# One plain load moved in front of three transposing transfers in the head of a GeGLU feed-forward kernel

## Chip, cores and metric

The kernel runs on one core of one Trainium2 chip. The metric is device time in microseconds (us), the median of several executions. The span of the profile is about 2 us shorter than that time.

## The reference

```python
# x: 32 x 32 x 1024 (1024 tokens), w_gate, w_up: 1024 x 3584, w_down: 3584 x 1024, all bf16
def reference(x, w_gate, w_up, w_down):
    return (gelu_tanh(x @ w_gate) * (x @ w_up)) @ w_down
```

## The kernel before

The kernel replaces matrix products by Strassen-like schemes with seven products. x is kept transposed in four quarters, b11, b12, b21, b22. VectorE (DVE) makes four sums of them, t1 to t4, and TensorE (PE) multiplies quarters and sums of x with quarters and sums of the weights; the sums of weight quarters are s1 to s4.

Until the first sum is there, PE works on "products ahead": gate rows (the tiles a12a and a12b) times b21, for six groups of four, results parked in SBUF. All but three of the earliest transfers of the head go through one queue, the sync engine's (SP). Its later part:

```python
for i in (0, 1):
    load_ahead(i, KQ, KD)
def load_halves(i):
    for k in range(0, KD, KQ):
        load_ahead(i, k, k + KQ)

load_halves(2)                 # gate rows of groups 2 to 4, 512 KB each in two loads
load_halves(3)
for which in (1, 0):
    load_w_all(0, which)       # w_up and w_gate of chunk 0
load_halves(4)
load_xT(0, 0, KD)              # b11: transposing transfer, 512 KB
load_xT(1, 0, KD)              # b12
load_ahead(5, 0, KD)           # gate rows of group 5, 512 KB, one plain load
load_xT(1, KD, DT)             # b22
for which in (1, 0):
    load_w_all(1, which)
```

The part that consumes them:

```python
group_ahead(4, "BBCC")
tt(t1, b12, b11, SUB)                                  # DVE
begun = []
for fl in range(FC):                                   # first product of chunk 0 reads b11
    psa = acc("A")
    prod(psa, quads(0, fl)[0], b11, True)
    begun.append((psa, added(ahead_at[fl], psa)))      # "c" on DVE
tt(t2, b22, t1, SUB)
group_ahead(5, "CCBB", between=lambda: nc.scalar.copy(b22r, b22))
...
tt(t3, b22, b12, SUB)
next(chunk0)                                           # s3 on DVE
tt(t4, b21, t2, SUB)
...
for ci in range(NCH):                                  # chunks of two feature tiles
    ...
    prod(psc[fl], s1[fl], t1, True)                    # needs t1
    ...
    prod(psa[fl], s2[fl], t2, False)                   # needs t2
    ...
    for st in open_fts:
        last_product(st)                               # adds on in the bank psa of the chunk before
    ...
    prod(psc[fl], s4[fl], b22r, False)
    h1.append(gelu(added(sn2[fl], psc[fl]), "h1", 2))  # "c" on DVE reads psc
    ...
    prod(psa[fl], s3[fl], t3, False)
    tt(g_of(ft)[:, NB:], added(sn5[fl], psa[fl]), h1[fl], MUL)   # "c" on DVE reads psa
```

In the text, c is the result of an `added`, and a bank is the piece of memory that a product adds up in (psA, psB or psC).

## Time and profile before

| | before |
|---|---|
| time, median of 3 at first | 274.03 us (273.82 to 274.19) |
| span of the profile | 272.0 us |
| PE busy | 266.5 us, 98% |
| last wait of PE for a transfer | ends at 4.70 us |

The page of the kernel before. In part 1 each engine has its busy time, share and number of instructions; part 4 gives shares of the chain of waits that ended last.

```profile
span 272.0 us, 3354 instructions
...
PE 266.5 (98%) x1182; PEld 191.4 (70%) x1198; DVE 193.3 (71%) x204; ACT 112.9 (41%) x185; POOL 118.6 (44%) x60
...
PE 97%; DMA 1%; issue 0%; ACT 0%; SPq 0%
```

The reader sees a kernel bound by PE. The chain's single DMA piece is the first weight tile.

The timeline of the kernel before on the sync queue: start, length of the issue, operation, tile. The length is the time in which the queue was busy or held up with issuing, not the transfer (the issue at 17.67 takes 0.58 us; its rows landed at 22.88).

```profile
8.95 2.08 SPq L208 DMA_DIRECT2D a12b<-in_w_gate_dram  x2
11.07 6.55 SPq L215 DMA_TRANSPOSE b<-in_x_dram  x2
17.67 0.58 SPq L208 DMA_DIRECT2D a12b<-in_w_gate_dram  x1
18.30 4.29 SPq L215 DMA_TRANSPOSE b<-in_x_dram  x1
22.64 0.58 SPq L135 DMA_DIRECT2D wu<-in_w_up_dram  x1
```

The timeline of the kernel before on DVE. The bracket gives the idle time in front and what ended it.

```profile
21.62 2.29 DVE L342 TENSOR_TENSOR t<-b,b 128x2048 fp32r<-128x2048 bf16 x1 [1.87 <-DMA b<-in_x_dram]
23.83 1.28 DVE L300 TENSOR_TENSOR c<-ahead,psA 128x512 f32<-128x512 f32 x2
25.03 2.29 DVE L348 TENSOR_TENSOR t<-b,t 128x2048 fp32r<-128x2048 bf16 x1
...
38.99 0.67 DVE L300 TENSOR_TENSOR c<-sn,psA 128x512 f32<-128x512 f32 x1
```

DVE waits 1.87 us for b12, then starts t1 (L342) and t2 (L348). There is no other bracket before 43 us: one delay of t1 moves all of this. The last line is the second `added` of chunk 0 that reads psA; it ends at 39.66.

The chain of the kernel before, in order of time: start, length, what.

```profile
25.93 1.73 PE psB L281 x8
27.66 1.85 PE psC L270 x8
29.50 1.82 PE psA L270 x8
```

At 27.66 the products with t1 start, at 29.50 those with t2. Nothing but PE stands there, so in this execution PE does not wait for a transfer there.

### The profile page before, as it was taken

Reading aid. Unit: us, or ns where it says so; the run is one execution under the profiler, and the core shown is the slowest. Engines: PE = TensorE matmul, PEld = TensorE weight load, DVE = VectorE, ACT = ScalarE, POOL = GpSimd, SP = SyncE. Lnnn points to the kernel's source line nnn. Section 1 sums busy time; section 2 is a strip of 40 time slices with the busy share of each in tenths; the row PEclk is TensorE's granted clock in tenths of the full one; section 3 lists DMA queues with packets and bytes.
Section 4 is the critical chain, followed back from the end, with each engine's and each line's share of the span. In section 5 each row is a group of like instructions: output and inputs, shape, how many; then the busy total and the mean of one; then the engine's idle time right before and its main releaser. Section 6 shows DMA issues by size and latency. Waiting matters only on the chain.

```text
span 272.0 us, 3354 instructions
## 1 busy us (share of the span) xinstructions
PE 266.5 (98%) x1182; PEld 191.4 (70%) x1198; DVE 193.3 (71%) x204; ACT 112.9 (41%) x185; POOL 118.6 (44%) x60
## 2 busy tenths in 40 slices
PE   7999999999999999999999999999999999999995
PEld 4444777877877878778778776764447888888883
DVE  1448998786685676765855556459999999999511
ACT  2435765355454643654546436430300023972001
POOL 1090099989787796796786966000000000000000
PEclk9999999999999999999999999999999999999999
DMA  7999130540523504505225090005992435686202
GB/s 170 324 263 254 32 113 15 145 133 23 157 68 86 155 17 140 142 12 157 84 72 154 22 322 7 0 2 157 350 302 80 138 132 186 219 280 205 78 0 77
DMA packets 55888, 35.86 MB, mean 132 GB/s; under 512 B 9792, under 2 KB 55872, under 8 KB 55872
## 3 DMA queue, kind: packets, MB, share of 16 engines
q1 hardware_dynamic: 52496, 33.10, 42.5%
q10 hardware_dynamic: 3376, 2.56, 2.9%
q8 instruction: 9, 0.15, 0.2%
q14 instruction: 7, 0.06, 0.1%
HBM read 31.72 MB, written 2.10 MB: 124 GB/s over the span
## 4 chain that ended last, share of the span: by engine, by line
PE 97%; DMA 1%; issue 0%; ACT 0%; SPq 0%
PE psA L270 37%; PE psC L270 19%; PE psA L419 18%; PE psC L419 7%; PE psB L419 7%; PE psB L281 3%; PE psC L281 3%; PE psA L281 2%; DMA a12a<-in_w_gate_dram 1%; PE psB L270 1%; ACT o_sb L559 0%; SPq L197 0%; PE tp L261 0%
## 5 line engine op out<-in xcount | busy, mean ns | idle before, releaser
L270 PE MATMUL psA<-t,s 128*128 128x512 f32 x224 | 58.3, 402 | 0.0
L245 ACT ACTIVATE h<-c 128x512 bf16<-128x512 f32 x56 | 34.3, 629 | 39.3 <-DVE c L300 39.3
L270 PEld LDWEIGHTS psA<-t,s 128*128 128x128 f32 x224 | 42.1, 188 | 9.9
L170 POOL TENSOR_TENSOR s<-wu 128x1024 fp32r<-128x1024 bf16 x13 | 29.4, 2262 | 32.7 <-DMA wu<-in_w_up_dram 28.3
L171 POOL TENSOR_TENSOR s<-s,wg 128x1024 fp32r<-128x1024 f32 x14 | 30.1, 2147 | 14.8 <-PE psA L270 13.7
L173 POOL TENSOR_TENSOR s<-wg,wu 128x1024 fp32r<-128x1024 bf16 x13 | 28.9, 2223 | 0.0
L270 PE MATMUL psC<-t,s 128*128 128x512 f32 x112 | 27.9, 391 | 0.0
L270 PE MATMUL psA<-t,a22r 128*128 128x512 f32 x112 | 27.9, 391 | 0.0
L270 PE MATMUL psC<-b22r,s 128*128 128x512 f32 x112 | 27.7, 389 | 0.0
L270 PE MATMUL psA<-b,wg 128*128 128x512 bf16 x102 | 25.6, 380 | 0.4
L305 ACT COPY sn<-psC 128x512 f32<-128x512 f32 x28 | 16.3, 588 | 23.3 <-PE psC L270 15.9
L270 PEld LDWEIGHTS psC<-t,s 128*128 128x128 f32 x112 | 21.0, 188 | 4.5
L270 PEld LDWEIGHTS psA<-t,a22r 128*128 128x128 f32 x112 | 21.0, 188 | 4.4
L270 PEld LDWEIGHTS psC<-b22r,s 128*128 128x128 f32 x112 | 21.0, 188 | 4.4
L300 DVE TENSOR_TENSOR c<-sn,psC 128x512 f32<-128x512 f32 x28 | 19.1, 687 | 6.6 <-PE psC L270 6.6
L300 DVE TENSOR_TENSOR c<-sn,psA 128x512 f32<-128x512 f32 x28 | 19.1, 682 | 6.4 <-PE psA L270 6.4
L318 DVE TENSOR_TENSOR hi<-h,psA 128x512 bf16<-128x512 bf16 x14 | 9.6, 688 | 18.0 <-PE psA L270 18.0
L270 PEld LDWEIGHTS <-wg 128*128 128x128 bf16 x128 | 11.4, 98 | 15.5 <-issue 3.7
L172 POOL TENSOR_TENSOR s<-wg,s 128x1024 fp32r<-128x1024 bf16 x10 | 21.5, 2150 | 0.8
L305 ACT COPY sn<-psA 128x512 f32<-128x512 f32 x32 | 18.4, 590 | 7.2 <-PE psA L270 7.1
L300 DVE TENSOR_TENSOR c<-ahead,psA 128x512 f32<-128x512 f32 x24 | 16.3, 686 | 3.7 <-PE psA L270 2.5
L398 DVE TENSOR_TENSOR lo<-c,h 128x512 bf16<-128x512 f32 x14 | 17.9, 1275 | 0.5
(90 smaller groups left out, 381.0 us busy)
## 6 DMA issues: line engine op xcount, KB each, us to landing
wu<-in_w_up_dram SPq DMA_DIRECT2D x14, 512.0 KB, 3.9
wdb<-in_w_down_dram SPq DMA_DIRECT2D x12, 512.0 KB, 4.7
wg<-in_w_gate_dram SPq DMA_DIRECT2D x9, 512.0 KB, 5.1
wdb<-in_w_down_dram SPq DMA_DIRECT2D x12, 384.0 KB, 4.3
v<-in_w_down_dram SPq DMA_DIRECT2D x4, 512.0 KB, 6.4
out_dram<-o_sb ACTq DMA_DIRECT2D x16, 128.0 KB, 1.7
a12b<-in_w_gate_dram SPq DMA_DIRECT2D x6, 256.0 KB, 5.5
wg<-in_w_gate_dram SPq DMA_DIRECT2D x6, 256.0 KB, 4.6
```

Source lines behind the costliest of these rows:

```text
L170: yield engs[0].tensor_tensor(s1, a21, a22, ADD)
L171: yield engs[1].tensor_tensor(s2, s1, a11, SUB)
L172: yield engs[2].tensor_tensor(s4, a12, s2, SUB)
L173: yield engs[3].tensor_tensor(s3, a11, a21, SUB)
L245: nc.scalar.activation(h, src, ACT.Gelu_apprx_tanh)
L270: nc.tensor.matmul(ps, lhsT=lhs[:, k, :], rhs=rhs[:, k, :], start=(start and k == 0), stop=(k == KD - 1), skip_group_check=True,)
L281: nc.tensor.matmul(ps[:, cols], lhsT=a12_ahead[i][:, k, j * P : (j + 1) * P], rhs=b21[:, k, cols], start=(k == 0 and not cols.start), stop ...
L300: tt(t, s, ps, ADD)
L305: nc.scalar.copy(t, ps)
L318: tt(g_of(ft)[:, :NB], h0, psa, MUL)
L398: tt(g_of(ft)[:, NB:], added(sn5[fl], psa[fl]), h1[fl], MUL)
L419: nc.tensor.matmul(banks[m], lhsT=lhs(k)[:, m * P : (m + 1) * P], rhs=rhs(k), start=(start and k == 0), stop=(k == HF - 1), skip_group_che ...
```

## The change

The intent is to let the gate rows of the products ahead load in one stretch, and then the three transposes of x follow each other.

```diff
+        def load_halves(i):
+            for k in range(0, KD, KQ):
+                load_ahead(i, k, k + KQ)
+
         def load_xT(nb, d0, d1):
 ...
-        def load_halves(i):
-            for k in range(0, KD, KQ):
-                load_ahead(i, k, k + KQ)
-
         load_halves(2)
         load_halves(3)
 ...
         load_halves(4)
+        load_ahead(5, 0, KD)
         load_xT(0, 0, KD)
         load_xT(1, 0, KD)
-        load_ahead(5, 0, KD)
         load_xT(1, KD, DT)
```

Only the sync queue's order differs. The instruction orders of PE, DVE, ACT and POOL are the same in both kernels.

## The prediction

> **What bounds the kernel now.** TensorE (PE). The page shows it busy 266.5 of 272.0 us (98%) at a granted clock of 9 tenths or more everywhere. The chain of waits has one DMA in it, the first weight tile until 4.65 us; from 4.70 to 268.83 us every piece is a matmul, apart from "issue" crumbs of 0.05 us. So a reordering of the head's transfers has no PE wait to remove. It can only use up slack.
>
> **What the change moves.** The streams of PE, VectorE (DVE), ACT and POOL are the same. On the sync queue one plain 512 KB load (gate rows of group 5) moves from third to first of four issues; the transposing transfers b11, b12, b22 then follow each other. Moving `load_halves` only moves a definition. Nothing is added or removed.
>
> Times before, from the timeline and the semaphore landings in the trace:
> - b11 issued 11.07, landed 17.71; PE uses it at 22.48.
> - b12 issued 15.72, landed 21.52, which ends DVE's idle time (1.87 us) before t1. 15 of its 16 completions came by 20.00; the last is 1.5 us late, just after a 16 KB packet of the instruction queue at 19.36 that took 1.12 us.
> - group 5's rows issued 17.67, landed 22.88; used at 24.20.
> - b22 issued 18.30, landed 24.65; t2 uses it at 25.03, the ACT copy b22r at 26.45.
>
> **Cost.** The DMA engines are saturated from 8 to 19 us (windows: 290 to 350 GB/s). 512 KB in front of b11 is about 1.5 us at that rate (estimate). I expect group 5's rows to land near 17.5, b11 near 19.2, b12 at 21.4 to 23.0[...], b22 at 23 to 24.7. [...]b12, group 5's rows and b22 landed in order of issue.
>
> **Critical path.** If b12 lands later by d, DVE, which runs without a gap from t1 at 21.62 to about 43 us, shifts by d. PE needs: t1 (ends 23.91, used 27.66, slack 3.7), t2 (ends 27.32, used 29.50, slack 2.1), t3 and s3 (end 29.5 and 30.65, used near 34.95), the psC banks freed by the adds at 33.90 (first ends 34.59, used 36.73, slack 2.1), chunk 1's s1 (slack 2.7), t4 (ends 32.86, used 40.35). The smallest slack is 2.1 us; I expect d of 0 to 1.5 us. So none of it reaches PE, and nothing is gained.
>
> **Prediction: 274.05 us, 273.6 to 274.6 eight times in ten.** Faster by over 2%: 0.3%; within 2%: 99.4%; slower by over 2%: 0.3%.
>
> **What would show the steps right.** The chain is again pure PE from 4.7 us on; the first fp32r products of psC (s1 by t1) and psA (s2 by t2) start at 27.7 and 29.5 as before; group 5's rows land 4 to 6 us earlier; b11 1 to 2 us later; t1 starts 0 to 1.5 us after 21.62; b22 lands no later. Wrong: a PE idle entry with DVE's t or a DMA as releaser, or t1 earlier than 21.5.
>
> **What would make it wrong.** d over 2.1 us: if the slow instruction packet hits b11 and the following transposes wait for it, b12 lands near 23.6 to 24 and PE stalls some tenths of a us at 29.5 or 36.7, below 0.5% of the time. The other way: [...]t1 might start earlier, which still gives PE nothing.

## The result, and the profile after

| | before | after |
|---|---|---|
| time, median of 6 | 273.92 us (273.42 to 274.50) | 274.13 us (273.54 to 274.46) |
| ratio, 95% interval | | 1.0006 (0.9988 to 1.0024) |
| span | 272.0 us | 272.1 us |

A ratio is the mean time of one kernel's fast runs over that of the other's of the same rounds, so it is not quite the ratio of the medians quoted here. The two kernels are the same within 0.25%.

The page of the kernel after:

```profile
span 272.1 us, 3354 instructions
...
PE 267.2 (98%) x1182; PEld 192.0 (71%) x1198; DVE 197.2 (72%) x204; ACT 112.3 (41%) x185; POOL 119.8 (44%) x60
...
PE 98%; issue 0%; ACT 0%; DVE 0%
```

The timeline of the kernel after on the sync queue and, in the next fence, on DVE:

```profile
9.46 2.53 SPq L208 DMA_DIRECT2D a12b<-in_w_gate_dram  x3
12.04 10.48 SPq L219 DMA_TRANSPOSE b<-in_x_dram  x3
22.56 0.58 SPq L135 DMA_DIRECT2D wu<-in_w_up_dram  x1
```

```profile
22.85 2.29 DVE L342 TENSOR_TENSOR t<-b,b 128x2048 fp32r<-128x2048 bf16 x1 [3.01 <-DMA b<-in_x_dram]
...
26.25 2.29 DVE L348 TENSOR_TENSOR t<-b,t 128x2048 fp32r<-128x2048 bf16 x1
...
40.23 0.68 DVE L300 TENSOR_TENSOR c<-sn,psA 128x512 f32<-128x512 f32 x1
```

DVE now waits 3.01 us for b12 instead of 1.87, and t1, t2 and c are all 1.2 us later. The chain of the kernel after at the same place:

```profile
26.01 1.73 PE psB L281 x8
27.74 1.86 PE psC L270 x8
29.60 1.82 PE psA L270 x8
```

PE starts the products with t1 and t2 within 0.1 us of where it did. It was already that much late at 12 us, long before t1, so this is not from the transposes.

When the transfers landed, read from the semaphore events in the traces (the last of the 16 completions of each transfer, us from the start of the span). "16 KB packet" is the start of a packet on the queue of kind "instruction", 0.9 to 1.2 us long:

| run | rows of group 5 | b11 | b12 | b22 | 16 KB packet | t1 starts |
|---|---|---|---|---|---|---|
| before | 22.88 | 17.71 | 21.52 | 24.65 | 19.36 | 21.62 |
| after | 17.77 | 21.08 | 22.75 | 24.89 | 18.98 | 22.85 |

The load in front came 5.1 us earlier, which nobody had waited for. b11 paid 3.4 us, b12 1.2 us, b22 0.2 us. So the change cost DVE 1.2 us and PE nothing. The delay of b12 is not the chance of two executions: in all five traces with this part of the queue as before (the kernel before and the runs with t1 three times or t3 twice, with warm-up) b12 landed at 21.19 to 21.61, in all three with the order of after at 22.35 to 22.75.

### The profile page after: what moved, and what is told of

Read it like the earlier page. It is cut to its first block, busy times and chain, and to the rows that moved or that the text cites. A ratio compares the mean times of both kernels' runs of the same rounds, so it can differ in the third digit from the quotient of the medians.

```text
span 272.1 us, 3354 instructions
## 1 busy us (share of the span) xinstructions
PE 267.2 (98%) x1182; PEld 192.0 (71%) x1198; DVE 197.2 (72%) x204; ACT 112.3 (41%) x185; POOL 119.8 (44%) x60
## 4 chain that ended last, share of the span: by engine, by line
PE 98%; issue 0%; ACT 0%; DVE 0%
PE psA L270 37%; PE psC L270 19%; PE psA L419 18%; PE psC L419 7%; PE psB L419 7%; PE psC L281 3%; PE psB L281 3%; PE psA L281 3%; PE psB L270 1%; PE psA L253 1%; PE tp L261 0%; ACT o_sb L559 0%; DVE b L264 0%
## 5 line engine op out<-in xcount | busy, mean ns | idle before, releaser
L170 POOL TENSOR_TENSOR s<-wu 128x1024 fp32r<-128x1024 bf16 x13 | 30.2, 2326 | 31.5 <-DMA wu<-in_w_up_dram 27.0
L398 DVE TENSOR_TENSOR lo<-c,h 128x512 bf16<-128x512 f32 x14 | 19.7, 1407 | 0.5
```

The costliest lines, as they stand in the source:

```text
L170: yield engs[0].tensor_tensor(s1, a21, a22, ADD)
```

## The experiments

The theory is that the order of the head's transfers moves only t1, and that PE has more slack behind t1 than the 1.2 us. There are two main rivals. One is that putting the transposes together is worth time by itself, which the load in front hides again. The other is that the change has no cost of its own at all.

Each timed run has runs of the kernel before on the same chip beside it. The first four that were made (group 5's rows last, one more load in front, and the two with t1 three times) share a before of 273.91 us (11 runs).

### Transposes together, group 5's rows last

The edit, against the kernel after:

```diff
         load_halves(4)
-        load_ahead(5, 0, KD)
         load_xT(0, 0, KD)
         load_xT(1, 0, KD)
         load_xT(1, KD, DT)
+        load_ahead(5, 0, KD)
```

> One part of the change alone: b11, b12, b22 follow each other, but nothing goes in front of them; group 5's rows go last. Theory (the order only moves slack): b11 lands near 17.7 as before, b12 at 20.0 to 21.5, b22 at 22 to 23, t1 starts no later than 21.7, no gain in time. Group 5's rows land at 24 to 25, needed at 24.2, so PE may wait up to 0.8 us there: 274.0 to 274.9. Rival (putting the transposes together is itself worth time, hidden in the change by the load in front): faster than before by 0.5 us or more.

Measured: 276.11 us (275.74 to 276.46), ratio 1.0073 (1.0042 to 1.0104). This is slower by 2.2 us, more than either side expected. The trace had a trap. PE's first products ran at half the rate of before. Three rows of the timeline of PE in this run:

```profile
5.61 0.63 PE L261 MATMUL tp<-ident,x_nat 128*128 128x128 bf16 x4
6.03 0.63 PE L281 MATMUL psC<-b,a12a 128*128 128x256 bf16 x2
6.46 0.63 PE L281 MATMUL psA<-b,a12a 128*128 128x256 bf16 x2
```

and the same stretch of PE's timeline in the kernel before:

```profile
5.23 0.40 PE L261 MATMUL tp<-ident,x_nat 128*128 128x128 bf16 x4
5.46 0.38 PE L281 MATMUL psC<-b,a12a 128*128 128x256 bf16 x2
5.68 0.38 PE L281 MATMUL psA<-b,a12a 128*128 128x256 bf16 x2
```

In the run with the rows last, rows of two matmuls follow each other every 0.43 us; in before, every 0.22 us. The slow spacing lasted until about 8.4 us; why is not shown by any run. The profile's granted clock does not show it: it is 1.00 from 4 to 8 us in both.

PE thus came 2 us late to everything. It was at group 5 at 26.18 us, when the rows had just landed (26.05), so no wait of PE for them shows. One trace could not tell the two causes apart.

> A second look at group 5's rows last. In its first profile PE ran its first products at half rate until 8.4 us and came 2 us late to everything, so that it met the late rows (landed 26.05) without waiting. Theory: the +2.2 us of its five runs is the late landing, not the half rate; if PE gets its full rate early this time, it comes to group 5 near 24.2 us and waits 1.6 to 2.1 us there for the gate rows, and the time is again 275.7 to 276.5. Rival (the half rate was the whole loss): with an early full rate the time is near 274 and no such wait shows.

Measured: 275.75 us, one run, with the full rate early (the first product of group 2 at 11.74 us, against 13.93 in the first look). The chain:

```profile
21.10 4.63 DMA a12b<-in_w_gate_dram
25.73 0.05 issue
25.78 1.90 PE psC L281 x8
```

PE waits for group 5's rows, and its list of waits has that one large entry:

```profile
PE psC L281 <- DMA a12b<-in_w_gate_dram: 1.8, 1, 1.8
```

This answers both questions. The loss is the late load; the half rate is not needed for it. And the transposes together gave nothing: b22 landed at 23.15 instead of 24.65, but t2 still started at 25.02, because DVE was busy with t1 and c until then. The span is 1.8 us longer than that of before (273.8 and 272.0), just the wait, so nothing was gained beside it.

### One more load in front

The edit, against the kernel after:

```diff
         load_ahead(5, 0, KD)
+        load_w_all(1, 1)
         load_xT(0, 0, KD)
         load_xT(1, 0, KD)
         load_xT(1, KD, DT)
-        for which in (1, 0):
-            load_w_all(1, which)
+        load_w_all(1, 0)
```

> The changed kernel with one more plain 512 KB load (chunk 1's w_up) in front of the three transposes. Theory (slack of 2.1 us on b12 through VectorE to t2; the change used 1.2): b12 lands near 24.5, t1 starts about 1.7 us after the changed kernel's 22.85, t2 ends near 30.3, and PE waits 0.3 to 1.6 us, mainly before the products with t2 near 29.6; time 274.4 to 275.7, best guess 274.9. Rival (there is more slack than read, or none is used): same as before within 0.2 us.

Measured: 275.38 us (275.15 to 276.07), ratio 1.005 (1.0024 to 1.0076). b12 landed at 23.84 and t1 started at 23.94, 1.1 us later than in the kernel after (1.7 were expected). PE's waits in this run, each with total, number and longest:

```profile
PE psA L270 <- DVE t L348: 0.4, 1, 0.4
PE psA L270 <- DVE c L300: 0.3, 1, 0.3
```

The first is the expected one, for t2 at 29.77. The second, at 42.05, was not on my list. It is the second `last_product` of chunk 0, which waits for the c that reads its bank. I had left this slack out. The timeline of PE in the kernel before (two lines) and in the kernel after (two lines):

```profile
40.19 1.98 PE L270 MATMUL psA<-t,a22r 128*128 128x512 f32 x8
42.00 1.98 PE L270 MATMUL psC<-b22r,s 128*128 128x512 f32 x8
...
40.27 1.98 PE L270 MATMUL psA<-t,a22r 128*128 128x512 f32 x8
42.09 1.98 PE L270 MATMUL psC<-b22r,s 128*128 128x512 f32 x8
```

In the kernel before, the eight matmuls of the two last products start at 40.19 and the next product at 42.00, so the second one starts at about 41.10; c ends at 39.66. That makes 1.4 us, less than the 2.1 us that I had called the smallest. In the kernel after, c ends at 40.91 and the product starts at about 41.18 (40.27 and half of 1.82): 0.3 us were left.

The two listed waits, 0.7 us, are less than what PE lost. The list counts idle time from the end of the last matmul, while matmuls overlap otherwise (eight take 1.98 us, but the next start 1.81 us after them). By starts, the product behind the second wait begins at 43.09 instead of 42.00: 1.1 us lost, and the spans (273.1 and 272.0) differ by as much.

### Is the slack there: t3 twice in the kernel before

The edit, against the kernel before (the expectation puts the slack at 1.6 us; the working above gives 1.4):

```diff
         tt(t3, b22, b12, SUB)
+        tt(t3, b22, b12, SUB)
```

> The kernel before, transfers untouched, with the subtraction t3 written twice (same result, 2.2 us more of VectorE, after t2, so t1 and t2 stay in time). New reading: the smallest slack is not at t2 but later, 1.6 us, where the second last_product of chunk 0 (near 41.3) waits for the add that reads the same bank (ends 39.66 in before). Then PE waits there 0.6 us[...]: 274.4 to 275.0, with VectorE's c as releaser near 41.3 to 42 us and no wait at 29.5. Rival (the prediction's list was complete, smallest slack 2.1 us): 273.9 to 274.1, no such wait.

Measured: 275.05 us (274.73 to 275.86), before 273.99 us, ratio 1.0039 (1.0019 to 1.0059). The transfers' order is that of before. The chain in its profile (an execution of 275.58 us, in which b22 landed at 25.46 and cost DVE a further 0.55 us before t2):

```profile
41.86 0.69 DVE c L300
42.55 0.04 issue
42.59 1.20 PE psA L270 x4
```

PE's waits for c in this run:

```profile
PE psC L270 <- DVE c L300: 0.9, 1, 0.9
PE psA L270 <- DVE c L300: 0.2, 1, 0.2
```

The wait for c at `last_product` is there, the second line. The first, 0.9 us at 37.50 for the psC bank that c frees, was not expected. It comes because the shift in this run was 2.9 us (c on psC at 36.76 instead of 33.90), above the 2.1 us of that slack. The rival (nothing below 2.1 us) still falls: the same c was 2.9 us late at `last_product`, where PE was by then 1.1 us late itself (its first `last_product` started at 41.30 instead of 40.19), so a slack of 2.1 us would have covered the rest and no second wait would show. So the run supports both slacks, but it is not the clean separation that I had planned.

### The cost of the change with no slack left

In both kernels t1 is computed three times (4.4 us more of DVE, same result):

```diff
         tt(t1, b12, b11, SUB)
+        tt(t1, b12, b11, SUB)
+        tt(t1, b12, b11, SUB)
```

On the kernel before:

> The kernel before, transfers untouched, with the subtraction t1 written three times (result the same, 4.4 us more of VectorE at the point where b12 has landed). Theory (slack 2.1 to 2.2 us before t2 and before the psC banks): PE waits 4.4 less 2.2, so +2.2 us (1.9 to 2.6): 276.2. Rival (VectorE's delay is absorbed elsewhere): below +1 us.

On the kernel after:

> The changed kernel with the same two extra subtractions, so that no slack is left on this chain. Theory: the change's hidden cost of 1.2 us (t1 at 22.85 instead of 21.62) now reaches PE whole: 1.0 to 1.5 us slower than the kernel before with the three subtractions, +3.5 us against before, 277.5. Rival (the change has no cost of its own, or group 5's earlier rows make it good): equal to the kernel before with the three subtractions within 0.3 us.

Measured: 276.84 us (275.50 to 277.61) for before, ratio 1.0095 (1.0062 to 1.0128), and 278.65 us (278.40 to 279.92) for after, ratio 1.0171 (1.0140 to 1.0202). PE's two longest waits in before with t1 three times (from its third look, told below; the first look has 1.3 us for each of the two, with another releaser named for the first of them):

```profile
PE psC L270 <- DVE t L344: 1.6, 1, 1.6
PE psA L270 <- DVE t L350: 1.3, 1, 1.3
```

and PE's waits in after with t1 three times:

```profile
PE psC L270 <- DVE t L344: 2.4, 1, 2.4
PE psA L270 <- DVE t L350: 1.3, 1, 1.3
```

With t1 three times, every run of after lies above every run of before, so the change does have a cost, and it shows as soon as no slack covers it. Its size is 1.0 us by the spans of the first two profiles (276.6 and 275.6), where t1 started at 22.83 and 21.71, and 1.8 us by the medians. The medians differ more because the six runs of before fell in two groups: three at 277.5 to 277.6, three at 275.5 to 276.2. The 1.0 us fits the expected 1.0 to 1.5; the 1.8 us does not.

Against the kernels without the extra sums, both expectations were too low: +2.9 us instead of +2.2 for before, +4.7 instead of +3.5 for after. Those sums used the slack of 2.1 us, not the 1.4 us at `last_product`. By the first profiles, c ended at 44.43 in before and at 45.54 in after, 4.8 and 5.9 us later than 39.66. Less 1.4 that is 3.4 and 4.5; the spans grew by 3.6 and 4.6. The median of before is no good test of this, as it lies between its two groups, where no run was.

> A second look at the kernel before with t1 three times, whose runs fell in two groups, 277.5 and 275.5 to 276.2. Theory: without slack on this chain, the 1.5 us that one instruction packet adds to b12's landing shows in the time. If this run is near 276, b12 lands near 20.1 with all 16 completions together and t1 starts near 20.2 to 20.8; if it is near 277.5, b12 lands near 21.6. Rival (the groups come from PE's first products at half or full rate): t1 starts at 21.7 in both, and the first product of group 2 stands later in the slow one.

Measured: 277.13 us, one run; b12 landed at 21.19, packet at 18.95. No run of the faster group was caught.

> A third look at the kernel before with t1 three times, on the chip of the run without warm-up. Theory: near 277.3 with b12 at 21.2 to 21.6 and the packet near 19.3; or near 276 with the packet after 20 us and b12 landed at 20.1.

Measured: 277.38 us, one run; b12 landed at 21.41, packet at 18.84. Again none of the faster group.

> The kernel before with t1 three times and without the 6 warm-up matmuls. Theory (the instruction packet is fetched when PE has issued some 180 of its instructions, in all ten traces between 172 and 189; what lies under it on the DMA engines lands 1.5 us late): PE [...]comes about 2 us late and has 12 instructions fewer behind it, so the packet comes near 22 us, after b12: b12 lands near 20.1, t1 starts 20.2 to 20.6, and as VectorE bounds this stretch the whole gets faster in spite of the slower start: 275.8 to 276.6. Rival (the fast runs of that kernel have another cause; a late PE is a loss): 277.5 to 279.5.

The edit is `NWARM = 6` to `NWARM = 0`. Measured: 277.57 us (277.14 to 278.11), before 273.65 us. Half of the expectation held. PE came 1.8 us late (DVE's last copy of its products in front of t1 starts at 20.88, in before at 19.06), the packet came at 24.68 (near 22 was expected), and b12 landed at 20.42 with all completions together, while b22, under the packet, landed at 26.93. But the time did not fall. The timeline of DVE in this run:

```profile
20.88 0.69 DVE L296 COPY ahead<-psA 128x512 f32<-128x512 f32 x1 [1.04 <-PE psA L281]
21.49 2.28 DVE L342 TENSOR_TENSOR t<-b,b 128x2048 fp32r<-128x2048 bf16 x1
```

PE was 1.8 us late, and DVE had a copy of PE's products in front of t1, so t1 waited for PE in place of b12. I had left that copy out of the sum. The cause of the faster group stays open.

### The kernel after

> A second look at the changed kernel for the spread of its transfers: time 273.5 to 274.5, b12 lands 21.4 to 23, PE never waits for VectorE's t or c, group 5's rows land near 17.5.

Measured: 273.97 us, one run. Group 5's rows landed at 17.17, b11 at 20.52, b12 at 22.35; t1 started at 22.45. PE had no wait for t or c. The picture of the first profile holds: t1 is 0.8 to 1.2 us later than before, and that is covered.

### What one instruction packet does to a transpose

The traces suggest why b11 paid 3.4 us and not the 1.5 us estimated for one load (512 KB at the 290 to 350 GB/s of the windows). A 16 KB packet of the instruction queue comes near 19 us as a rule (18.84 to 19.36 in five of the seven traces quoted here), and again each time PE has issued some 220 to 290 more of its instructions (in the kernel before, instructions of PE in the trace that had started by then: 180, 413, 669, 926; some may be missing from the trace). By their lists of waits, PE has none at these times in before, after and the two looks at "transposes together"; the transposing transfers in flight landed late:

| run | packet at | transfer in flight then | its 16 completions | the next transfers |
|---|---|---|---|---|
| before | 19.36 | end of b12 | 15 by 20.00, the last at 21.52 | b22 24.65 |
| after | 18.98 | b11 | 6 by 19.59, 10 from 20.79 to 21.08 | b12 22.75 |
| transposes together, first look | 21.92 | b22 | 16 from 24.31 to 24.51 | b12, ahead of it, landed at 20.61 |
| transposes together, second look | 19.30 | b12 | 15 from 21.32 to 21.36, the last at 21.52 | b22 23.15 |
| t1 three times, no warm-up | 24.68 | end of b22 | 15 by 25.44, the last at 26.93 | |

The two looks at "transposes together" are the same program. In one the packet came 2.6 us later, because PE had started slowly: b12 landed 0.9 us earlier and b22 1.4 us later. In after, the packet caught b11, and the packets of all transposes almost stopped from 20.0 to 20.7 us: about 10 in each quarter of a microsecond, against 280 normally. This is a reading of the traces: late landings go with the packet in all of them, but no run took the packet away.

No run points to a version that beats both kernels: PE has no wait for these transfers that an order could remove.

## Why the prediction was right, point by point

- **PE bounds the head, and no order of these transfers can gain.** Right for the orders that were run. The chain after the change is PE again, and the times are 273.92 and 274.13 us. Transposes together by themselves gained nothing; b22's 1.5 us went unused.
- **A load in front makes the transposes behind it later.** Right in sign: b11 landed 3.4 us, b12 1.2 us and b22 0.2 us later. In both kernels the transfers landed in the order of their issue (before: b11 17.71, b12 21.52, rows 22.88, b22 24.65; after: rows 17.77, b11 21.08, b12 22.75, b22 24.89). Group 5's rows were expected near 17.5 and landed at 17.77 and 17.17.
- **b11 near 19.2, "1 to 2 us later".** Wrong: 21.08 and 20.52, 2.8 to 3.4 us later. The estimate took 1.5 us for the load alone (at the windows' rate of 290 to 350 GB/s, which held until 17 us; from 17 to 19 us the windows show 235 and 246). The instruction packet, which had come on b12 in the kernel before (19.36 us), came on b11 (18.98 us). That this did no harm was luck in part: b11 had 4.8 us until PE's use of it, but t1 reads it too, 3.9 us after it landed.
- **b12 at 21.4 to 23.0, d of 0 to 1.5 us.** Right: 22.75 and 22.35, d of 1.2 and 0.8 us. That d was less than the 1.5 us estimated for the load fits b12 no longer having the packet on it; no run isolates this.
- **b22 "no later".** Level: 24.89 and 24.54, against 24.65.
- **"The smallest slack is 2.1 us".** Wrong. The `last_product` that waits for c has 1.4 us. The conclusion stood because d was 1.2 us, but with 0.3 us left, not 0.9. My stated limit for a stall, d over 2.1 us, was too generous.
- **A stall would be small, some tenths of a us.** With d of 2.3 us (one more load in front) PE lost 1.1 us by its starts and by the spans, and the time was 1.5 us longer by the medians. The estimate was low: it had one stall at t2 in it, and the second, at `last_product`, was not on the list.

## What to carry to other kernels

When the chain of waits is one engine's work from end to end, reordering transfers has slack to spend and no wait to remove (here the change spent 1.2 us of 1.4 us at `last_product`, and the times are 273.92 and 274.13 us); ask how much, and list every consumer behind the delayed tile, also those that only free a bank. A change that measures as "same" may have used up nearly all of that slack: a copy of both kernels with the slack filled (here t1 three times) shows its hidden cost. Check in each trace that the matmuls' spacing is normal before a delay is explained by transfers, as a slow start can cover a wait (here 0.43 us instead of 0.22 in one look, and no wait for the late rows in its list; 1.8 us of wait in the other).
